# Linear attention on one core: every product as 64x64 quarters of TensorE, four shared double PSUM banks, a new order of the stages

## The chip, the cores and the metric

The kernel runs on one core of one Trainium2 chip. The metric is the device time of one execution in microseconds (us). Four computing engines work side by side: TensorE (PE in the profile, with its weight loads listed apart as PEld), VectorE (DVE), ScalarE (ACT) and GpSimd (POOL). SyncE (SP) issues DMA transfers. Each engine runs its own list of instructions in order and waits on semaphores for the others. TensorE writes its products to PSUM, a small memory of banks; DVE and ACT read PSUM and the larger SBUF.

## The reference

```
def phi(x):
    proj = np.einsum('bhsd,df->bhsf', x, w_phi)
    proj = proj - np.max(np.abs(proj), axis=-1, keepdims=True)
    return np.concatenate([np.exp(proj), np.exp(-proj)], axis=-1)
q_p, k_p = (phi(q), phi(k))
kv = np.einsum('bhsf,bhsd->bhfd', k_p, v)
z = np.sum(k_p, axis=2)
num = np.einsum('bhsf,bhfd->bhsd', q_p, kv)
den = np.einsum('bhsf,bhf->bhs', q_p, z)[..., None] + 1e-06
return (num / den).astype(np.float32)
```

q, k and v are 8 batches x 8 heads x 576 rows x 64 columns, w_phi is 64x128, so a row has 256 features. The attention output is laid out as 4608 tokens x 512 and goes through a mixture of 8 experts (512 to 1024, ReLU, back to 512). Tokens are assigned to experts greedily by descending logit, at most 576 tokens to an expert.

## The kernel before, in words

The attention stage takes about the first 355 us of the execution, the routing the next 45, and the experts the rest. The change touches the attention stage alone.

The stage is cut into 16 **units**, one for each pair of batches (bp) and pair of heads (hp); four units in a row share a pair of batches. A unit's steps, with the names that the text uses and the lines of the profile:

- loads of q, k and v by SP's DMAs (L113), ten in a unit;
- kt and qt: three groups each of three 128x128 transposes of k and q on PE (L165, L243), copied from PSUM to SBUF by ACT (kh at L166, qh at L244);
- kg and qg: three groups each of projections with w_phi, as 64x64 quarters of PE's array (L152). On DVE follow the maximum of the absolute values (km, qm at L156) and the subtraction (ks, qs at L159), on ACT for the keys two exponentials (ke, L177 and L178);
- kv: the key-value products (L189 with 128 rows of the array, L194 with quarters), copied by ACT (L212), then bd, quarter products that lay the result out for the next step and append the gate (L222), copied by ACT (kz, L225);
- the sums over rows of the key features on POOL (L201, L202, L205), then z, their sums over partitions on PE (L234, one column each), copied by DVE into kz (zk, L235);
- T: three groups of six transposes of the query features (L255), then two exponentials on ACT (ex, L258);
- num: four groups of the numerator, the denominator and eight gate columns (L279, 73 columns, in groups of 5, 4, 5 and 4 blocks of rows). On DVE follow what the text calls an x group, x0 to x3: add 1e-6 to the denominators (L283), reciprocals (L284), gate columns (lg, L288), and the output rows (L298). For every fourth unit lg is summed into the logits L (L291, L293). After x3 the rows go out by DMA (L301).

In the last unit the output rows are multiplied by ACT (L296). After every fourth unit but the last come twelve short steps of routing preparation on DVE (L433 to L473, called chores here) and a count on PE (L469). Forty steps that set up routing constants run on DVE and POOL in the first units.

The order of the work is set by a planner, the class Plan: each step is a task with an engine, a duration, a due time, the tasks it depends on, and the buffers it takes and gives back. The planner picks, engine by engine, the ready task with the lowest cost of due time and waiting. It counts a switch between shapes of PE's array as extra time. The due times come from the table ATT. The order is fixed when the kernel is built, and each engine runs it as written.

PSUM holds two double banks D (projections, bd and T), two single banks S (transposes, z, num and the count) and two banks for kv.

Of the kernel before, what the change touches and what calls it, by code (L numbers as in the profile page):

```python
# [17 lines left out]
class Plan:  # L18
# [9 lines left out]
    def order(self):  # L28
# [7 lines left out]
        while left:  # L36
            best=None; horizon={}
            cand={}
            for x in left:
# [4 lines left out]
                if not ok: continue
                for d_ in x['deps']:
                    y=self.by[d_]
                    if 'end' not in y: ok=False; break
                    r=max(r,y['end']+self.SEM if e!='PE' or y['eng']!='PE' else y['start']+y['dur'])
                if not ok: continue
                for kind,n,u in x['slot']:  # L50
                    h=held.setdefault(kind,[0.]*n)
                    z=[t for t in h if t is not None]
                    if not z: ok=False; break
                    r=max(r,min(z)+self.SEM)
                if not ok: continue
                cand.setdefault(e,[]).append((r,x))
# [33 lines left out]
def attention(ctx, tc, nc, q, k, v, w_phi, w_gate, xs, L, C, xp, cfg={}, after=None, later=None, count=None, init=iter(())):  # L90
# [3 lines left out]
    d=dict(TI=21.,kt=-4.,kg=0.,kv=4.,bd=4.,z=5.,zc=6.,qt=6.,qg=10.,T=2.5,num=26.,stay=2.,ks=4.,qs=4.,ns=5.,ng=6,ld=60.,nqP=8,init=25.,pitch=1.)  # L94
# [11 lines left out]
    def load(u,first=lambda: None):
        bp,hp=divmod(u,NP)
        qi=sb.tile([128,2,9,D],F32,name='qi',bufs=2); ki=sb.tile([128,2,9,D],F32,name='ki',bufs=2); vi=sb.tile([128,2,9,D],F32,name='vi',bufs=3)
        T['q',u],T['k',u],T['v',u]=qi,ki,vi
        def put(t,p,s0,s1,x,b,row):  # L110
# [25 lines left out]
    QI=227.  # L136
    def unit(u):
        bp,hp=divmod(u,NP)
        t0=u*d['TI']
# [4 lines left out]
        def slots(*l): return tuple((kd,n,(kd,u) if len(z)==0 else (kd,u)+tuple(z)) for kd,n,*z in l)
        ld0=('ld',)

        def project(x,X,src,i0,i1):
            p=X['p']=bank(X['b'],[128,2,512])(x)
# [12 lines left out]
        for g in range(3):  # L161
            def pe(x,g=g):
                if g==0: T['kh',u]=sb.tile([128,9,128],F32,name='kh',bufs=2)
                p=T['ktp',u,g]=bank(('S',u,'kt',g),[128,3,128])(x)
                for i in range(3): PE.transpose(p[:,i],ch(T['k',u],3*g+i),ident)  # L165
            def act(x,g=g): A.copy(T['kh',u][:,3*g:3*g+3],T['ktp',u,g])  # L166
            due=d['kt']+d['ks']*1.5*g
            add(('kt',g),'PE',327.,due,pe,ld0,'A',slots(('S',NS,'kt',g),*((('kh',2),) if g==0 else ())),(('ki',u),),after=(5500.,9000.,10000.)[g] if u==0 else 0.)
            add(('kh',g),'ACT',ac(384),due+.4,act,(('kt',g),),frees=(('S',u,'kt',g),))
        for g in range(3):  # L170
# [8 lines left out]
            add(('kg',g),'PE',3*QI,due,pe,[('kh',g)],'Q',slots(('D',ND_,'kg',g)),(('kh',u),),after=8000. if u==0 else 0.)  # L179
            add(('km',g),'DVE',dv(768),due+.8,lambda x,X=X: maxima(X,'km',3),(('kg',g),))  # L180
            add(('ks',g),'DVE',dv(768),due+1.4,lambda x,X=X: differ(X,'kt',3),(('km',g),),slot=slots(('ktt',3,g)),frees=(('D',u,'kg',g),))
            add(('ke',g),'ACT',2*ac(768,False),due+2.,act,(('ks',g),),slot=slots(('kP',2)) if g==0 else (),frees=(('ktt',u,g),))
        for g in range(2):
            def pe(x,g=g):
                kP=T['kP',u]; v_=T['v',u]
                if g==0: T['kvps',u]=[ps.tile([128,256],F32,name='kv%d'%i,bufs=1) for i in range(2)]
                for i,b in KV[g]:
                    a,s_=divmod(b,9); c=a^i
                    PE.matmul(T['kvps',u][i][64*c:64*c+64,:],v_[:,a,s_,:],kP[:,b,:],start=b in (0,5,9,14),stop=False,skip_group_check=True)  # L189
                if g==1:  # L190
                    for a in range(2):
                        for i in range(2):
                            c=a^i; r=slice(64*i,64*i+64)
                            PE.matmul(T['kvps',u][i][64*c:64*c+64,:],v_[r,a,4,:],kP[r,9*a+4,:],start=False,stop=True,skip_group_check=True)  # L194
            add(('kv',g),'PE',4*430.+(530. if g==1 else 0.),d['kv']+d['ks']*(2+2.5*g),pe,[('ke',1+g)]+([('kv',0)] if g else []),('B','Q') if g else 'B',slots(('kv',1)) if g==0 else (),(('kP',u),('vi',u)))
# [30 lines left out]
        add(('bd',),'PE',560.,kend+d['bd'],bdp,[('kvt',)],'Q',slots(('D',ND_,'bd')))  # L226
        add(('kz',),'ACT',ac(576),kend+d['bd']+.6,kzc,[('bd',)],frees=(('D',u,'bd'),),slot=slots(('kz',2)))
        def z(x):
            p=T['zp',u]=bank(('S',u,'z'),[128,8])(x)
            for i in range(2):  # L230
                for fh in range(2):
                    for a in range(2):
                        n=4*i+2*fh+(a^i)
                        for e in range(2): PE.matmul(p[64*e:64*e+64,n:n+1],T['ks',u][:,i,a,128*fh+64*e:128*fh+64*e+64],C['one'][:,0:1],start=True,stop=True,skip_group_check=True)  # L234
# [4 lines left out]
        for g in range(3):
            def pe(x,g=g):  # L240
                if g==0: T['qh',u]=sb.tile([128,9,128],F32,name='qh',bufs=2)
                p=T['qtp',u,g]=bank(('S',u,'qt',g),[128,3,128])(x)
                for i in range(3): PE.transpose(p[:,i,:],ch(T['q',u],3*g+i),ident)  # L243
            def act(x,g=g): A.copy(T['qh',u][:,3*g:3*g+3],T['qtp',u,g])  # L244
            due=d['qt']+d['qs']*1.5*g
            add(('qt',g),'PE',327.,due,pe,ld0,'A',slots(('S',NS,'qt',g),*((('qh',2),) if g==0 else ())),(('qi',u),),after=10500. if u==0 else 0.)
            add(('qh',g),'ACT',ac(384),due+.4,act,[('qt',g)],frees=(('S',u,'qt',g),))
        for g in range(3):
# [3 lines left out]
            def tr(x,X=X,g=g):  # L252
                p=X['T']=bank(('D',u,'T',g),[128,2,512])(x)
# [636 lines left out]
```

## Time and profile before

| what | value |
|---|---|
| median of 3 runs | 857.91 us (857.84 to 860.48) |
| the profiled execution's own time | 857.9 us |
| its span | 856.1 us (1.8 us of its time lie around it) |
| granted TensorE clock, mean | 0.978 |
| busy over the span | PE 803.4, DVE 570.2, ACT 370.0, POOL 262.1 us |
| first bd of units 3, 7 and 11 (middle of the stage) | 100.24, 182.31, 264.36 us |
| last num of PE ends | about 355 us |

The three times of bd say that a cycle of four units takes 82.07 and 82.05 us. In the rows of the timeline a line gives the start, the duration, the engine, the line of the kernel, the operation, what is written and read, the shapes, the count (x24 stands for 24 records in a row), and in brackets the idle time of the engine before it and what ended it. A group's line gives busy time and mean duration of one.

### The profile page before, as it was taken

The page shows a single profiled execution, that of the slowest core. Times are in us where ns is not written, and L with a number is a line of the kernel's source. Part 1 is how long each engine was busy: PE and PEld are TensorE (multiplying, and loading weights), DVE is VectorE, ACT ScalarE, POOL GpSimd, SP SyncE. Part 2 cuts the span into 40 slices and gives each one's busy share as a digit, 9 for nine tenths or more (in the row PEclk, how much of TensorE's full clock was granted, in tenths as well). Part 3 has the DMA queues.
Part 4 walks back from the last instruction along what each step waited for, and adds up shares of the span by engine and source line. Part 5 has one row for each costly group of instructions (what it writes and reads, how often), then busy time and mean ns, then how long its engine had stood idle before and what let it go on. Part 6 is the DMA issues. An engine that isn't in the chain of part 4 may idle for free.

```text
span 856.1 us, 24776 instructions
## 1 busy us (share of the span) xinstructions
PE 803.4 (94%) x10508; PEld 685.8 (80%) x10508; DVE 570.2 (67%) x1534; ACT 370.0 (43%) x691; POOL 262.1 (31%) x300
## 2 busy tenths in 40 slices
PE   4879999999999999758999999999999999999995
PEld 2768887887788878658979879889889798898984
DVE  1787788778867887577858658668667577461410
ACT  1646665566566565413334324333333243251410
POOL 1654455555555555111040130310301202401001
PEclk9999999999999999958999999999999999999999
DMA  8424444454445421134143340532233225610301
GB/s 170 116 54 113 114 114 126 118 135 121 117 120 134 117 58 31 57 114 131 54 147 118 129 147 35 177 131 95 97 118 123 83 104 185 214 63 38 118 13 43
DMA packets 73534, 91.88 MB, mean 107 GB/s; under 512 B 5280, under 2 KB 56512, under 8 KB 73424
## 3 DMA queue, kind: packets, MB, share of 16 engines
q1 hardware_dynamic: 67328, 71.32, 29.3%
q0 software_dynamic: 6096, 18.98, 6.5%
q8 instruction: 83, 1.36, 0.7%
q14 instruction: 27, 0.22, 0.1%
HBM read 71.40 MB, written 18.87 MB: 105 GB/s over the span
## 4 chain that ended last, share of the span: by engine, by line
PE 69%; issue 16%; DVE 7%; POOL 4%; DMA 2%; ACT 1%; SPq 0%; POOLq 0%; DVEq 0%; ACTq 0%
PE h L763 19%; PE y L792 16%; PE S L279 7%; PE D L152 6%; PE kv L189 4%; PE D L255 3%; PE y L807 2%; PE S L165 2%; PE S L243 2%; PE h L739 2%; PE S L234 2%; DVE km L156 1%; PE rps L530 1%; POOL out_dram L821 1%; DVE kt L159 1%
## 5 line engine op out<-in xcount | busy, mean ns | idle before, releaser
L763 PE MATMUL h<-xh,w1h 128*128 128x272 f32 (+1 forms) x512 | 145.9, 305 | 0.7 <-ACT xh L740 0.7
L763 PE MATMUL h<-xh,w1l 128*128 128x304 f32 (+1 forms) x512 | 143.9, 301 | 0.0
L774 ACT ACTIVATE fh<-h 128x272 fp32r<-128x272 f32 (+1 forms) x128 | 49.2, 384 | 134.5 <-PE h L763 122.1
L821 POOL DMA_INDIRECT out_dram<-ysb,idx x40 | 40.5, 1012 | 207.0 <-ACT ysb L815 203.5
L792 PE MATMUL y<-w2h,fl 128*128 128x512 f32 x256 | 102.0, 398 | 0.0
L792 PE MATMUL y<-w2l,fh 128*128 128x512 f32 x256 | 101.9, 398 | 0.0
L792 PE MATMUL y<-w2h,fh 128*128 128x512 f32 x256 | 101.5, 396 | 0.0
L763 PEld LDWEIGHTS h<-xh,w1h 128*128 128x128 f32 x512 | 97.2, 190 | 2.5 <-issue 1.2
L763 PEld LDWEIGHTS h<-xh,w1l 128*128 128x128 f32 x512 | 97.4, 190 | 0.0
L734 POOL DMA_INDIRECT xg<-xs,idx x40 | 40.0, 1000 | 178.2 <-issue 141.5
L763 PE MATMUL h<-xl,w1h 128*128 128x272 f32 (+1 forms) x512 | 91.4, 298 | 0.0
L778 DVE SCALAR_TENSOR_TENSOR fl<-h,fh 128x272 fp32r<-128x272 f32 (+1 forms) x128 | 52.8, 419 | 55.6 <-ACT fh L774 41.9
L201 POOL TENSOR_TENSOR ks<-kP 128x512 f32<-128x512 f32 x32 | 40.9, 1277 | 157.1 <-issue 130.2
L279 PE MATMUL S<-kz,qP 128*64 128x73 f32 x2304 | 87.4, 230 | 1.0 <-ACT xp L296 1.0
L279 PEld LDWEIGHTS S<-kz,qP 128*64 128x64 f32 x2304 | 78.1, 137 | 11.0 <-issue 9.1
L202 POOL TENSOR_TENSOR ks<-ks,kP 128x512 f32<-128x512 f32 x64 | 81.5, 1273 | 4.9
L258 ACT ACTIVATE qP<-D 128x768 f32<-128x768 f32 x96 | 72.5, 808 | 9.1 <-PE D L255 5.6
L763 PEld LDWEIGHTS h<-xl,w1h 128*128 128x128 f32 x512 | 75.5, 188 | 0.0
L815 ACT COPY ysb<-y 128x512 f32<-128x512 f32 (+1 forms) x40 | 21.8, 544 | 104.4 <-PE y L792 72.3
L156 DVE TENSOR_REDUCE km<-D 128x6 f32<-128x768 f32 x48 | 45.7, 953 | 29.4 <-PE D L152 29.2
L189 PE MATMUL kv<-kP,vi 128*64 128x256 f32 x512 | 60.9, 379 | 0.0
L156 DVE TENSOR_REDUCE qm<-D 128x6 f32<-128x768 f32 x48 | 45.6, 950 | 20.0 <-PE D L152 19.8
(177 smaller groups left out, 1550.5 us busy)
## 6 DMA issues: line engine op xcount, KB each, us to landing
raww<-in_moe_w_dram SPq DMA_DIRECT2D x64, 512.0 KB, 5.5
qi<-in_q_dram SPq DMA_DIRECT2D x32, 288.0 KB, 4.6
xs<-xp SPq DMA_DIRECT2D x16, 576.0 KB, 3.8
ki<-in_k_dram SPq DMA_DIRECT2D x32, 160.0 KB, 3.8
vi<-in_v_dram SPq DMA_DIRECT2D x32, 160.0 KB, 5.2
ki<-in_k_dram SPq DMA_DIRECT2D x32, 128.0 KB, 3.7
vi<-in_v_dram SPq DMA_DIRECT2D x32, 128.0 KB, 5.0
xg<-xs,idx POOLq DMA_INDIRECT x40, 3.5
```

Of the source, the lines that this page charges most:

```text
L152: PE.matmul(p[64*(c^r):64*(c^r)+64,r,128*(i-i0):128*(i-i0)+128],src[64*r:64*r+64,i,64*(c^r):64*(c^r)+64],C['w'][64*r:64*r+64,:],start=True ...
L156: V.tensor_reduce(m[:,:,0:n],X['v'],axis=AX.X,op=OP.max,apply_absolute_value=True)
L189: PE.matmul(T['kvps',u][i][64*c:64*c+64,:],v_[:,a,s_,:],kP[:,b,:],start=b in (0,5,9,14),stop=False,skip_group_check=True)
L201: if i==0: G.tensor_add(ks[:,:,a],X(0),X(1))
L202: elif i<3: G.tensor_add(ks[:,:,a],ks[:,:,a],X(i+1))
L258: for fh in range(2): A.activation(qP[:,fh].rearrange('p (b i) f -> p b (i f)',b=2),X['T'][:,:,0:384],AF.Exp,scale=1.0-2*fh)
L279: PE.matmul(p[64*ab:64*ab+64,j-j0,:],T['qP',u,jj][:,fh,o,64*ab:64*ab+64],T['kz',u][:,ab,fh,a^ab,:],start=fh==0,stop=fh==1)
L763: PE.matmul(p,ws[:,k,o:o+128],xx[:,k,o1:o2],start=n==0,stop=n==11)
L774: A.activation(hh[:,f,o1:o1+m1],p[:,0:m1],AF.Relu)
L778: V.scalar_tensor_tensor(hl[:,f,o1:o1+m1],p[:,0:m1],0.0,hh[:,f,o1:o1+m1],op0=OP.max,op1=OP.subtract)
L792: PE.matmul(p,hx[:,f,o:o+128],ws[:,f%2,:],start=n==0,stop=n==23)
L821: st=G.indirect_dma_start(out=ov,out_offset=bass.IndirectOffsetOnAxis(ap=iv,axis=0),in_=yv,in_offset=None)
```

## The change

- All transposes, kv, z and num become 64x64 quarter products, as the projections and bd were. A transpose of 128x128 becomes four quarter products with the identity, of 64 columns each (new function turn, L131). A quarter product reads one half of the 128 rows, so where a sum runs over 128 rows the two row halves go to the two banks of a double bank, and are added afterwards.
- For kv, ACT copies one half (kvc, L220) and DVE adds the other (kvt, L223). For z, DVE copies one half and adds the other (L252). For num, ACT copies one half to a new SBUF tile nu (xc, L301), and DVE adds the other half into it (L304).
- The rest of an x group reads nu in SBUF instead of PSUM (L306, L307, L311). The multiplication that gives the output rows goes from DVE to POOL (xa, L320), in the last unit too.
- PSUM is four double banks D0 to D3, which all products share.
- Loads are tasks of their own for k, q and v (L114), where one task issued all ten.
- The planner has new costs and a new table of due offsets for each step, with corrections for the first and the last unit. The order on every engine is new.

The core of the diff:

```
-    ND_,NS=2,2
+    ND_=4
+    def turn(p,g,f):
+        for i in range(3):
+            for c in range(2):
+                for r in range(2): PE.matmul(p[64*c:64*c+64,r,64*i:64*i+64],f(i)[64*r:64*r+64,64*c:64*c+64],ident[64*r:64*r+64,64*r:64*r+64],start=True,stop=True,skip_group_check=True)
...
-                for i in range(3): PE.transpose(p[:,i],ch(T['k',u],3*g+i),ident)
-            def act(x,g=g): A.copy(T['kh',u][:,3*g:3*g+3],T['ktp',u,g])
+                turn(p,g,lambda i: ch(T['k',u],3*g+i))
+            def act(x,g=g): A.copy(rows(T['kh',u][:,3*g:3*g+3]),halves(T['ktp',u,g],3))
...
+                def mm(i,b,r,start,stop):
+                    a,s_=divmod(b,9); c=a^i; z=slice(64*r,64*r+64)
+                    PE.matmul(T['kvps',u][64*c:64*c+64,r,256*i:256*i+256],v_[z,a,s_,:],kP[z,b,:],start=start,stop=stop,skip_group_check=True)
...
+        def kvc(x):
+            T['kvT',u]=sb.tile([128,2,256],F32,name='kvT',bufs=2)
+            A.copy(T['kvT',u].rearrange('p i f -> p (i f)'),T['kvps',u][:,0])
         def kvt(x):
-            kt=T['kvT',u]=sb.tile([128,2,256],F32,name='kvT',bufs=2)
-            for i in range(2): A.copy(kt[:,i],T['kvps',u][i])
+            kt=T['kvT',u].rearrange('p i f -> p (i f)')
+            V.tensor_add(kt,kt,T['kvps',u][:,1])
...
-                                PE.matmul(p[64*ab:64*ab+64,j-j0,:],T['qP',u,jj][:,fh,o,64*ab:64*ab+64],T['kz',u][:,ab,fh,a^ab,:],start=fh==0,stop=fh==1)
+                                for r in range(2):
+                                    h=slice(64*r,64*r+64)
+                                    PE.matmul(p[64*ab:64*ab+64,r,m:m+73],T['qP',u,jj][h,fh,o,64*ab:64*ab+64],T['kz',u][h,ab,fh,a^ab,:],start=fh==0,stop=fh==1,skip_group_check=True)
+                def half(x,n=n,X=X):
+                    X['t']=sb.tile([128,5,73],F32,name='nu',bufs=3)
+                    A.copy(X['t'].rearrange('p j n -> p (j n)')[:,0:73*n],X['p'][:,0,0:73*n])
...
-                    V.tensor_scalar(rd[:,:n],p[:,:n,72:73],1e-6,None,op0=OP.add)
+                    V.tensor_add(f,f,X['p'][:,1,0:73*n])
+                    rd=X['rd']=sb.tile([128,5,1],F32,name='rd',bufs=4)
+                    V.tensor_scalar(rd[:,:n],t[:,:n,72:73],1e-6,None,op0=OP.add)
                     V.reciprocal(rd[:,:n],rd[:,:n])
...
-                    V.tensor_mul(lg[:,j0:j1,:,h],p[:,:n,64:72],rd[:,:n].to_broadcast([128,n,8]))
+                    V.tensor_mul(lg[:,j0:j1,:,h],t[:,:n,64:72],rd[:,:n].to_broadcast([128,n,8]))
...
-                        V.tensor_mul(x_[:,j0:j1,64*a:64*a+64],p[:,:n,0:64],rd[:,:n].to_broadcast([128,n,64]))
+                def pool(x,a=a,j0=j0,j1=j1,n=n,X=X,g=g):
+                    x_=T['x',u]
+                    G.tensor_mul(x_[:,j0:j1,64*a:64*a+64],X['t'][:,:n,0:64],X['rd'][:,:n].to_broadcast([128,n,64]))
...
-ATT = {'TI': 20.56, 'kt': -4.44, 'kg': -1.69, 'kv': 7.48,
...
+ATT = {'TI': 26.229, 'kt': -4.44, 'kg': -1.69, 'kv': 7.48,
...
```

The order shows three places. The first is TensorE at the start of the stage. Names are the tiles written and read: ki_96 and ki_119 are the keys of units 0 and 1 before, ki_97 and ki_113 those after, kh the copied transposes, w the projection weights. Before:

```order
L165 MATMUL S0_132<-ident_69,ki_96 128x128 [waits DMAHW0_49,DMAHW1_49,DVE_49,PE_49]
L165 MATMUL S0_132<-ident_69,ki_96 128x128
L165 MATMUL S0_132<-ident_69,ki_96 128x128 [waits DMAHW3_49,DMAHW2_49]
L165 MATMUL S1_137<-ident_69,ki_119 128x128 [waits DMAHW3_49,DMAHW2_49]
L165 MATMUL S1_137<-ident_69,ki_119 128x128
L165 MATMUL S1_137<-ident_69,ki_119 128x128 [waits DMAHW5_49,DMAHW4_49]
L152 MATMUL D0_143<-w_65,kh_131 64x128 [waits DMASW0_49,Activation_49]
```

And after:

```order
L131 MATMUL D0_119<-ident_69,ki_97 64x64 [waits DMAHW2_49]
L131 MATMUL D0_119<-ident_69,ki_97 64x64 [waits DMAHW3_49]
L131 MATMUL D0_119<-ident_69,ki_97 64x64
L131 MATMUL D1_132<-ident_69,ki_97 64x64 x12
L131 MATMUL D2_146<-ident_69,ki_97 64x64 x12
L160 MATMUL D3_160<-w_65,kh_118 64x128 [waits DMASW0_49,Activation_49]
L160 MATMUL D3_160<-w_65,kh_118 64x128 x11
```

The first projection stood behind transposes of unit 1's keys; now it stands behind transposes of unit 0's keys alone.

The second place is VectorE in the middle of the stage: the last x group of a unit and what follows it. S1 and D1 are PSUM banks, nu, rd, lg and xp are SBUF tiles. Before:

```order
L283 TENSOR_SCALAR rd_2343<-S1_2310 128x4 [waits PE_49]
L284 RECIPROCAL rd_2343<-rd_2343 128x4 [waits DVE_49]
L288 TENSOR_TENSOR lg_2033<-S1_2310,rd_2343 128x32 [waits DVE_49]
L298 TENSOR_TENSOR xp_2032<-S1_2310,rd_2343 128x4x64
L156 TENSOR_REDUCE km_2364<-D1_2330 128x6 [waits PE_49]
```

And after, with the end of the x group before it:

```order
L311 TENSOR_TENSOR lg_5802<-nu_7021,rd_7059 128x40 [waits DVE_49]
L304 TENSOR_TENSOR nu_7081<-nu_7081,D1_7023 128x292 [waits Activation_49]
L306 TENSOR_SCALAR rd_7097<-nu_7081 128x4 [waits DVE_49]
L307 RECIPROCAL rd_7097<-rd_7097 128x4 [waits DVE_49]
L311 TENSOR_TENSOR lg_5802<-nu_7081,rd_7097 128x32 [waits DVE_49]
L164 TENSOR_REDUCE km_7136<-D2_7104 128x6 [waits PE_49]
L167 TENSOR_TENSOR kt_7178<-D2_7104,km_7136 128x2x3x128 [waits DVE_49]
```

The x groups of a unit now stand one behind the other, their operands are SBUF tiles but for the bank of the first add, and the multiplication is gone from this engine.

At the same place GpSimd had only the sums of the key features (ks and kP are SBUF tiles):

```order
L201 TENSOR_TENSOR ks_2382<-kP_2227 128x2x256 [waits PE_49,Activation_49,Pool_49]
L202 TENSOR_TENSOR ks_2382<-ks_2382,kP_2227 128x2x256 [waits Pool_49] x2
L205 TENSOR_TENSOR ks_2382<-ks_2382,kP_2227 64x256 [waits Pool_49]
L205 TENSOR_TENSOR ks_2382<-ks_2382,kP_2227 64x256
L201 TENSOR_TENSOR ks_2382<-kP_2227 128x2x256 [waits Activation_49,Pool_49]
```

And it has now, in the unit of the VectorE rows above:

```order
L210 TENSOR_TENSOR ks_6911<-ks_6911,kP_6766 128x2x256 [waits Pool_49]
L320 TENSOR_TENSOR xp_6997<-nu_6947,rd_6994 128x5x64 [waits DMAHW2_49,DVE_49]
L320 TENSOR_TENSOR xp_6997<-nu_6999,rd_7003 128x4x64 [waits DVE_49]
L320 TENSOR_TENSOR xp_6997<-nu_7021,rd_7059 128x5x64 [waits DVE_49]
L210 TENSOR_TENSOR ks_6911<-ks_6911,kP_6766 128x2x256 [waits Pool_49]
L320 TENSOR_TENSOR xp_6997<-nu_7081,rd_7097 128x4x64 [waits DVE_49]
L213 TENSOR_TENSOR ks_6911<-ks_6911,kP_6766 64x256 [waits Pool_49] x2
```

The four multiplications stand between the sums. On TensorE at this place, after the last num of the unit (D3, kz, qP), the rows run:

```order
L298 MATMUL D3_7606<-kz_7101,qP_7304 64x73 x31
L234 MATMUL D0_7647<-bd_103,kvT_7444 64x72 [waits DVE_49]
L131 MATMUL D1_7667<-ident_69,qi_6538 64x64 [waits Activation_49]
L160 MATMUL D2_7689<-w_65,kh_7122 64x128 [waits DVE_49]
L131 MATMUL D0_7708<-ident_69,ki_6660 64x64 [waits Activation_49]
L131 MATMUL D3_7723<-ident_69,ki_6660 64x64 [waits DVE_49]
L131 MATMUL D1_7737<-ident_69,qtt_7328 64x64 [waits Activation_49]
L160 MATMUL D0_7768<-w_65,kh_7707 64x128 [waits Activation_49]
L131 MATMUL D3_7785<-ident_69,ki_6660 64x64 [waits Activation_49]
L131 MATMUL D2_7800<-ident_69,qtt_7343 64x64 [waits DVE_49]
```

These are the first instructions of num3's remainder, bd, a qt, a kg, two kt, a T, a kg, a kt and a T; rows that follow each in the same bank are left out. The bank D2 of the last T was that of the kg six rows above it.

More of the change, by code (lines that the diff above doesn't have):

```diff
@@ L49, in order @@
                 if not ok: continue
+                want={}
                 for kind,n,u in x['slot']:
[L51 to L54, printed above, removed]
+                    h=held.setdefault(kind,[0.]*n); i=want[kind]=want.get(kind,-1)+1
+                    z=sorted(t for t in h if t is not None)
+                    if i>=len(z): ok=False; break
+                    r=max(r,z[i]+self.SEM)
                 if not ok: continue
@@ L74, in order @@
                 m0=x['mode'][0]
-                if mode[0] not in (None,m0): s+=95.
-                if mode[0]!=m0 or s>free.get(e,0.)+1.: s+=100. if m0=='A' else 50.
+                if mode[0] not in (None,m0): s+=self.swc
+                if mode[0]!=m0 or s>free.get(e,0.)+1.: s+=self.swA if m0=='A' else self.swO
                 mode[0]=x['mode'][-1]
@@ L101, in attention, with load, put @@
     w=sb.tile([128,512],BF,name='warm',bufs=1); V.memset(w,0.0)
-    p=ps.tile([128,512],F32,name='S0',bufs=1)
-    for _ in range(cfg.get('nwarm',7)): PE.matmul(p,w[:,0:128],w,start=True,stop=True)
+    p=ps.tile([128,2,512],F32,name='D0',bufs=1)
+    for _ in range(cfg.get('nwarm',7)): PE.matmul(p[:,0],w[:,0:128],w,start=True,stop=True)
     T={}
     HS=S*D
[L106 to L110, printed above, removed]
+    def load(u,n,first=lambda: None):
+        bp,hp=divmod(u,NP); b=2*bp
+        x=dict(q=q,k=k,v=v)[n]
+        t=T[n,u]=sb.tile([128,2,9,D],F32,name=n+'i',bufs=3 if n=='v' else 2)
+        def put(p,s0,s1,b,row):
             n=s1-s0
@@ L241, in pe, with act @@
                 if g==0: T['qh',u]=sb.tile([128,9,128],F32,name='qh',bufs=2)
-                p=T['qtp',u,g]=bank(('S',u,'qt',g),[128,3,128])(x)
-                for i in range(3): PE.transpose(p[:,i,:],ch(T['q',u],3*g+i),ident)
-            def act(x,g=g): A.copy(T['qh',u][:,3*g:3*g+3],T['qtp',u,g])
+                p=T['qtp',u,g]=bank(('D',u,'qt',g))(x)
+                turn(p,g,lambda i: ch(T['q',u],3*g+i))
+            def act(x,g=g): A.copy(rows(T['qh',u][:,3*g:3*g+3]),halves(T['qtp',u,g],3))
             due=d['qt']+d['qs']*1.5*g
-            add(('qt',g),'PE',327.,due,pe,ld0,'A',slots(('S',NS,'qt',g),*((('qh',2),) if g==0 else ())),(('qi',u),),after=10500. if u==0 else 0.)
-            add(('qh',g),'ACT',ac(384),due+.4,act,[('qt',g)],frees=(('S',u,'qt',g),))
+            add(('qt',g),'PE',3*QT,due,pe,[*lq]+[('qt',g-1)]*(g>0),'Q',slots(('D',ND_,'qt',g),*((('qh',2),) if g==0 else ())),(('qi',u),))
+            add(('qh',g),'ACT',ac(384),due+.4,act,[('qt',g)],frees=(('D',u,'qt',g),))
         for g in range(3):
@@ L301, in dve @@
                         nc.sync.dma_start(o,x_)
-                add(('num',a,g),'PE',n*270.,due,pe,[('zk',)]+[('ex',j) for j in js],'B',slots(('S',NS,'num',a,g)),tuple(('qP',u,j) for j in js)+(('kz',u),))
-                add(('x',a,g),'DVE',70+70+dv(8*n)+(dv(64*n) if u<NU-1 else 0)+(250 if hp==NP-1 else 0),due+1.6,dve,[('num',a,g)],frees=(('S',u,'num',a,g),))
+                add(('num',a,g),'PE',n*270.,due,pe,[('zk',)]+[('ex',j) for j in js],'Q',slots(('D',ND_,'num',a,g)),tuple(('qP',u,j) for j in js)+(('kz',u),))
+                add(('xc',a,g),'ACT',ac(73*n),due+1.2,half,[('num',a,g)],slot=slots(('nu',3,a,g)))
+                add(('x',a,g),'DVE',dv(73*n)+70+70+110+8*n+(250 if hp==NP-1 else 0),due+1.6,dve,[('xc',a,g)]+[('x',*divmod(i-1,2))]*(i>0)+[('x',1,1,u-1)]*(i==0 and hp>0),frees=(('D',u,'num',a,g),))
+                add(('xa',a,g),'POOL',150+2.*64*n,due+2.,pool,[('x',a,g)]+[('xa',*divmod(i-1,2))]*(i>0),frees=(('nu',u,a,g),))
         if hp==NP-1 and u<NU-1:
```

114 lines of the change are left out of this document (58 added, 56 removed).

## The prediction

> **What bounds the kernel now.** I read the busy time by stretches first, then the chain of waits, then the timeline of one unit. The first rows are the middle of the attention stage (PE, PEld, DVE, ACT, POOL, each with its busy us and count) and the chain's shares by engine.
>
> ```profile
> 60.00:340.00 280.00, 273.97 (x5922) 228.87 (x5924) 222.53 (x478) 175.26 (x287) 143.19 (x136) 1.00 0.43 108
> PE 69%; issue 16%; DVE 7%; POOL 4%; DMA 2%; ACT 1%; SPq 0%; POOLq 0%; DVEq 0%; ACTq 0%
> ```
>
> PE is busy 273.97 of 280 us at full clock; DVE is busy 222.53, so 79%, POOL 51%. The stage is bound by PE with DVE not far behind. The next rows are PE in one unit, start and duration first.
>
> ```profile
> 80.54 0.68 PE L222 MATMUL D<-bd,kvT 64*64 64x72 f32 x32
> 81.15 1.10 PE L234 MATMUL S<-one,ks 128*64 128x1 f32 x32
> 82.17 0.89 PE L152 MATMUL D<-w,kh 64*64 64x128 f32 x24
> 82.99 0.55 PE L165 MATMUL S<-ident,ki 128*128 128x128 f32 x3
> 83.38 0.49 PE L243 MATMUL S<-ident,qi 128*128 128x128 f32 x3
> 83.70 0.82 PE L255 MATMUL D<-ident,qtt 128*128 128x128 f32 x6
> 84.45 1.24 PE L279 MATMUL S<-kz,qP 128*64 128x73 f32 x32
> 85.61 0.89 PE L152 MATMUL D<-w,kh 64*64 64x128 f32 x24
> 86.32 0.83 PE L152 MATMUL D<-w,qh 64*64 64x128 f32 x24
> 87.09 1.49 PE L279 MATMUL S<-kz,qP 128*64 128x73 f32 x40
> 88.40 1.90 PE L189 MATMUL kv<-kP,vi 128*64 128x256 f32 x16
> 90.23 0.55 PE L243 MATMUL S<-ident,qi 128*128 128x128 f32 x3
> ...
> 95.41 0.66 PE L194 MATMUL kv<-kP,vi 64*64 64x256 f32 x8
> 95.89 0.83 PE L152 MATMUL D<-w,kh 64*64 64x128 f32 x24
> ...
> 100.24 0.55 PE L222 MATMUL D<-bd,kvT 64*64 64x72 f32 x24
> 162.61 0.68 PE L222 MATMUL D<-bd,kvT 64*64 64x72 f32 x32
> ```
>
> From bd to bd this unit takes 100.24 - 80.54 = 19.70 us, and four units 162.61 - 80.54 = 82.07. So a cycle has 82.07 - 4x19.70 = 3.27 us more, which go with the chores of its last unit. Durations overlap at their ends, so I price by start to start.
>
> **The change on PE.** A projection behind another of the same shape takes 86.32 - 85.61 = 0.71, ahead of a num 87.09 - 86.32 = 0.77, and ahead of transposes 82.99 - 82.17 = 0.82. The 32 records of num ahead of a projection take 1.16, where the 40 ahead of kv (same shape) take 1.31, which makes 1.05 of 32. So a switch of shape costs 0.06 to 0.11, say 0.10. I count 13 in the unit; with one shape they all go, 1.3 us.
>
> The price of a quarter comes from bd: 16 products in 0.61, 0.51 without its switch, so 0.127 for four quarters of 72 columns. Num becomes 36 such fours, 4.6; its rows give 2x1.31 + 2x1.05 = 4.7. Three transposes become three fours of 64 columns, at most 0.38; rows 0.39 and 0.32. A T of six becomes at most 0.76; row 0.75. L189's 16 records (eight half-array products) take 1.83 with a switch, 0.43 for two, so 3.87 for nine fours of 256 columns against 2x1.83 + 0.48 = 4.14 with switches. Z goes from 32 records to 64: by bd's 0.51/32 = 16 ns a record it takes 1.0, by its own present 1.02/32 = 32 ns a record 2.0. I take 1.0, since bd's shape is the new one. PE's own work per unit: 6x0.37 + 3x0.75 + 6x0.71 + 3.87 + 0.51 + 1.0 + 4.6 = 18.7. That agrees with 19.70 - 1.3 = 18.4. I take 18.6; the bounds are 18.4 and 19.4 (z at its present rate). The quarters gain the switches and little else.
>
> **The change on DVE.** It loses the multiplication of four x groups and gains four adds, kvt and a second zk. These rows give the prices, by the spacing of starts.
>
> ```profile
> 87.45 0.95 DVE L156 TENSOR_REDUCE qm<-D 128x6 f32<-128x768 f32 x1
> 88.31 0.95 DVE L159 TENSOR_TENSOR kt<-D,km 128x768 f32<-128x768 f32 x1
> 89.18 0.95 DVE L159 TENSOR_TENSOR qtt<-D,qm 128x768 f32<-128x768 f32 x1
> 90.04 0.16 DVE L283 TENSOR_SCALAR rd<-S 128x5 f32<-128x5 f32 x1
> 90.23 0.19 DVE L284 RECIPROCAL rd<-rd 128x5 f32<-128x5 f32 x1
> 90.46 0.23 DVE L288 TENSOR_TENSOR lg<-S,rd 128x40 f32<-128x40 f32 x1
> 90.58 0.48 DVE L298 TENSOR_TENSOR xp<-S,rd 128x320 f32<-128x320 f32 x1
> ```
>
> 768 elements take 0.87 where nothing is waited for, and about 0.1 more where a maximum is followed by its own subtraction. The add of 365 or 292 elements lies between L288 and L159, about 0.45 or 0.37 by size; with 0.19 + 0.23 + 0.23 for the rest, an x group of five or four takes 1.09 or 0.99. Kvt with 512 elements is 0.58.
>
> Now the loop that can set the pace. Between the end of a unit's last qg and the T that waits for bank D2, DVE in its new order has qm, kvt, qs, four x groups, km and ks: 1.0 + 0.58 + 0.87 + 2x1.09 + 2x0.99 + 1.0 + 0.95 + 0.15 for the signal = 8.7. PE has four nums, bd, two qt, two kg, three kt and a T there: 4.6 + 0.51 + 5x0.37 + 2x0.71 + 0.75 = 9.1. That kg on D2 needs the add of x2, and the T needs the ks of that kg, so PE can't run ahead of DVE. The rest of the unit is 18.6 - 9.1 = 9.5 of PE. A unit is thus 9.5 plus the longer of 9.1 and 8.7 + c, where c is what DVE waits inside that chain. At c = 0 PE sets it, 18.6.
>
> **What c is.** The x groups read SBUF now, and POOL, which had only sums, has four multiplications more, which fall among them. The rows show what a DVE instruction with SBUF operands does beside POOL.
>
> ```profile
> 108.71 2.63 POOL L202 TENSOR_TENSOR ks<-ks,kP 128x512 f32<-128x512 f32 x2
> 110.16 0.23 DVE L288 TENSOR_TENSOR lg<-S,rd 128x40 f32<-128x40 f32 x1
> 110.70 0.73 DVE L293 SCALAR_TENSOR_TENSOR L<-L,lg 128x40 f32<-128x40 f32 x1
> 111.42 1.53 POOL L205 TENSOR_TENSOR ks<-ks,kP 64x256 f32<-64x256 f32 x2
> 114.38 2.63 POOL L202 TENSOR_TENSOR ks<-ks,kP 128x512 f32<-128x512 f32 x2
> 116.08 1.00 DVE L293 SCALAR_TENSOR_TENSOR L<-L,lg 128x32 f32<-128x32 f32 x1
> 117.08 1.51 POOL L205 TENSOR_TENSOR ks<-ks,kP 64x256 f32<-64x256 f32 x2
> 121.03 0.23 DVE L293 SCALAR_TENSOR_TENSOR L<-L,lg 128x40 f32<-128x40 f32 x1
> ...
> 132.10 1.66 POOL L205 TENSOR_TENSOR ks<-ks,kP 64x256 f32<-64x256 f32 x2
> 133.10 0.70 DVE L449 TENSOR_SCALAR dg<-di 128x9 bf16<-128x9 int32 x1
> ...
> 356.95 0.16 DVE L449 TENSOR_SCALAR dg<-di 128x9 bf16<-128x9 int32 x1
> ```
>
> L293 has two SBUF inputs. Beside L202 it takes 0.73 and 1.00, and both times it ends as L202 ends (110.70 + 0.73 = 111.43, and 108.71 + 2.63 = 111.34; 117.08 and 117.01). With POOL idle the same shape takes 0.23. L449, a scalar operation from SBUF to SBUF, takes 0.70 beside L205 and 0.16 alone. L288, with one input in PSUM, takes 0.23 beside L202. So a DVE instruction of the first two kinds that meets a POOL instruction waits for its end. In the new x group these are L306 (was from PSUM) and L311 (was PSUM and SBUF).
>
> The Trainium skill states this rule ("SBUF — State Buffer", Who interferes with whom): the port pair that DVE shares with GpSimd is held for a whole instruction, two SBUF inputs contend for it, and the scalar form too where it takes both ports. The rows agree. By that rule, as by the rows, the change puts eight such instructions into each unit.
>
> POOL's durations are 2.63/2 = 1.3 for 512 elements and 1.53/2 = 0.75 for 256, so about 0.87 and 0.75 for the multiplications of 320 and 256. Its busy time per unit becomes 2x(3x1.3 + 2x0.75) + 2x(0.87 + 0.75) = 14.0, 70% of a unit. The multiplication of a group starts when its reciprocal is done and about as its lg ends, and the next group's L306 comes 0.45 to 0.5 later, behind the add: a wait of 0.3 to 0.4 in three of the groups and 0.3 behind a sum in the first, 1.3 together. Between the third and fourth multiplication stands a sum of 1.3; if it starts between L306 and L311 of x3, L311 waits 1.1, and I count half, 0.5. So c = 1.8. Below, it is 0 if nothing overlaps; above, 3 and more if several L311 wait for a sum. The unit then takes 9.5 + 8.7 + 1.8 = 20.0, 0.3 more than now.
>
> **The start, the chores, the tail.**
>
> ```profile
> 9.19 0.45 PE L165 MATMUL S<-ident,ki 128*128 128x128 f32 x1 [1.67 <-DMA ki<-in_k_dram]
> ...
> 15.64 0.66 PE L165 MATMUL S<-ident,ki 128*128 128x128 f32 x2 [6.00 <-DMA ki<-in_k_dram]
> ...
> 17.34 1.56 PE L152 MATMUL D<-w,kh 64*64 64x128 f32 x24
> 18.96 0.96 DVE L156 TENSOR_REDUCE km<-D 128x6 f32<-128x768 f32 x1 [14.60 <-PE D L152]
> ```
>
> PE waited 6.00 us for unit 1's keys ahead of the first projection, and DVE began at 18.96. In the new order nothing of unit 1 stands there. With unit 0's keys in at 9.19, the copy (0.5) and the projection follow, and DVE begins at about 11: -8. It is up to -10 if early waits for loads go too, and only -3 if the values, now issued behind both queries and unit 1's keys, hold kv back. Loads are ten issues on SP as before, and in the middle PE waits for none of the rows above.
>
> The chores and L293 fall into DVE's chain, which has no slack left: for a cycle I take 6 us in place of 3.27, from four L293 at up to 1.00, and two L291 and twelve short steps beside them. Over the three cycles with chores that is +8 (0 if they find gaps, +13 if each waits as L449 did). At the end, the last output rows come by a copy, an add and a POOL multiplication in place of ACT's: +2 (0 to 4). The copies of num's halves go to ACT, which is busy 175.26 of 280: four a unit at no more than L298's 0.48 each add 1.9 to some 12.3, and are covered; the add of a group starts that much later, which the order allows for by putting other work of DVE ahead of it.
>
> Sum, against the profiled execution's 857.9 (which is the median 857.91): -8 + 14x0.3 + 8 + 2 = +6, so 864. The break-even is where 14x(18.2 + c - 19.70) = -2, at c = 1.36. A measurement of this kernel can tell about 0.3%, 2.6 us.
>
> **The rivals.**
> - No wait to speak of (the other side, faster). If POOL runs in DVE's PSUM instructions, or few of the eight meet it, c stays under 0.4 and PE sets the pace at 18.6 to 18.8. Then -8 + 14x(18.7 - 19.70) + 4 + 2 = -16: 842, from 838 to 846. For it: no row shows L306 in this place, and an instruction may slip in between two of POOL's. Against: POOL at 70%. Chance 0.22.
> - Half of it: only L311 waits, or L306 alone, c = 1.0. The unit is 19.2, and the sum -8 - 7 + 7 + 2 = -6: 852, from 848 to 856. It decides below c = 1.36. Chance 0.20.
> - More of it: several L311 behind sums, c = 3. The unit is 21.2: -8 + 21 + 9 + 2 = +24, 882. For it: L293 waited 0.5 and 0.8 in two cases of three. Chance 0.14.
> - The change doesn't do what it says on PE: small quarters are bound by issue, not by columns. Z has 32 ns a record with one column now, bd 16 with 72. Turns, num and z are 288 + 288 + 64 = 640 records in the new unit, 10.2 us at bd's rate. At the mean of the two rates, 24 ns, they take 15.4, the unit 18.6 + 5.1 = 23.7, and the sum is -8 + 56 + 8 + 2 = +58: 916. Bd's own 32 records of quarters speak against it, so its chance is 0.05. The Trainium skill ("TensorE: Matmul & The Clock Gate", Back-to-back issue gap) puts a floor of about 25 ns under the spacing for up to 64 columns; by it the same sum gives an estimate of about 925. Bd's 0.61/32 = 19 ns, its switch included, lies below that floor.
>
> **How the numbers follow.** The forecast, c from 1.4 to 2.4, has 0.39 and a range of 858 to 872. Faster by over 0.3% (under 855.3) takes all of the first rival and 0.16 of the second: 0.38. Within 0.3% (855.3 to 860.5) takes the rest of the second, 0.04, and 0.08 of the forecast: 0.12. Slower takes 0.50. The range leaves out the last rival and the outer parts of the first and third: 838 to 882. The likeliest case's own range, since cases of both signs hold most of the chance, is 858 to 872.
>
> **What would show it.** Right: bd to bd about 20.0 in units without chores, PE waiting for DVE ahead of a T or kg, L306 or L311 at several times 0.16 and 0.23 and ending with a POOL instruction, no switch costs (a projection at 0.71 everywhere), the first DVE maximum near 11 us. Wrong: L306 and L311 near their old 0.16 and 0.23 (then the first rival), PE busy the whole unit at over 19 us (then the quarters cost more), or waits of PE for ACT or DMAs, which no term here has.

## The result and the profile after

The changed kernel takes 964.75 us (962.7 to 966.36, four runs) against 858.13 us, a ratio of 1.1234 with an interval of 1.1204 to 1.1265. (Every ratio below, too, is to runs of the kernel before that were made beside it.) That is slower by 107 us and far outside the stated range. The profiled execution took 965.38 us with a span of 963.6.

The whole loss lies in the attention stage: the last num of PE starts at 460.14 us of the span where it started at 354.75, and from there to the end it is 503.4 us against 501.4. The first row is a stretch of the changed kernel's attention stage, in the columns of the prediction.

```profile
60.00:440.00 380.00, 281.42 (x11972) 259.87 (x11968) 242.02 (x498) 195.25 (x323) 178.53 (x191) 0.96 0.29 79
```

From its page, the queue that loads instructions (packets, MB, share) and the chain's shares:

```profile
q8 instruction: 140, 2.29, 1.0%
PE 67%; issue 22%; DVE 6%; POOL 3%; DMA 1%; ACT 1%; SPq 0%; POOLq 0%; DVEq 0%; ACTq 0%
```

PE is busy 281.42 of 380 us, 74%, where it was 98%. No other engine is busier than it was: DVE 64%, POOL 47%. So no engine is full, and yet hardly a wait for another engine stands in the profile: the waits of PE in the same stretch (total, times, longest) name "issue", which is time in which the engine waited for nothing that the profile shows.

```profile
PE D L131 <- issue: 35.1, 18, 3.0
PE D L160 <- issue: 29.2, 20, 2.8
PE D L298 <- issue: 26.5, 21, 2.1
PE D L197 <- issue: 2.0, 2, 1.3
```

That is 93 us in 61 stops, most of them of 1 to 3 us. Over the whole attention stage it is 108 us, as much as the kernel lost; in the kernel before it was 0.2. The granted clock in this stretch was 0.96 against 1.00 in the middle of the kernel before; the run wide_turn below has 0.99 there and takes as long, so the clock isn't the cause. The timeline of PE shows where they fall.

```profile
193.32 1.92 PE L298 MATMUL D<-kz,qP 64*64 64x73 f32 x105 [1.37 <-issue]
195.03 0.52 PE L131 MATMUL D<-ident,qi 64*64 64x64 f32 x22
197.22 0.21 PE L131 MATMUL D<-ident,qi 64*64 64x64 f32 x1 [1.68 <-issue]
197.23 0.29 PE L298 MATMUL D<-kz,qP 64*64 64x73 f32 x3
197.28 0.22 PE L131 MATMUL D<-ident,qi 64*64 64x64 f32 x1
197.33 1.18 PE L298 MATMUL D<-kz,qP 64*64 64x73 f32 x61
198.30 0.71 PE L234 MATMUL D<-bd,kvT 64*64 64x72 f32 x32
198.80 0.56 PE L131 MATMUL D<-ident,qi 64*64 64x64 f32 x24
199.14 0.43 PE L160 MATMUL D<-w,kh 64*64 64x128 f32 x6
200.95 0.70 PE L160 MATMUL D<-w,kh 64*64 64x128 f32 x17 [1.37 <-issue]
```

The stops fall in the middle of groups, where no step begins or ends. Between the stop at 197.22 and that at 200.95 stand 1 + 3 + 1 + 61 + 32 + 24 + 6 = 128 records; between 193.32 and 197.22 it is 105 + 22 = 127. Each record has its own weight load, so this is 256 instructions. The instruction queue moved 2.29 MB in 140 packets, 16 KB each, and PE's 2 x 17868 instructions make 139.6 blocks of 256. The kernel before had 83 packets, and 2 x 10508 / 256 = 82.1:

```profile
q8 instruction: 83, 1.36, 0.7%
```

The packets of that queue beside the stops, all from the trace of the changed kernel:

```
code load, us         PE's last product begins            PE goes on
190.65 to 191.78      191.72                              193.32
194.45 to 195.77      195.32                              197.22
198.33 to 199.74      199.31                              200.95
203.42 to 204.69      203.28                              206.05
207.20 to 208.19      208.17                              209.67
```

PE goes on 1.2 to 1.5 us after a load has ended, and the next load begins about 1.1 us later, in all but one of the rows. With 1.0 to 1.4 us for the load itself that makes a loop of some 3.8 us, one block at a time. All 62 stops of over 0.8 us in the attention stage lie like that: PE goes on 1.2 to 1.7 us after the end of a load, and from one stop to the next there are one to five times 128 records, less up to 5 (other instructions may take places in a block). In the attention stage of the changed kernel the loads follow each other at a median of 3.83 us, the closest 5% at under 3.48. In the kernel before the median is 5.73 and the closest 3.55.

### The profile page after: what moved, and what is told of

The parts are those of the page before. It is cut to its first block, busy times and chain, and to the rows that moved or that the text cites. A ratio compares the mean times of both kernels' runs of the same rounds, so it can differ in the third digit from the quotient of the medians.

```text
span 963.6 us, 39526 instructions
## 1 busy us (share of the span) xinstructions
PE 815.1 (85%) x17868; PEld 726.5 (75%) x17868; DVE 600.1 (62%) x1570; ACT 393.0 (41%) x721; POOL 303.9 (32%) x364
## 3 DMA queue, kind: packets, MB, share of 16 engines
q8 instruction: 140, 2.29, 1.0%
## 4 chain that ended last, share of the span: by engine, by line
PE 67%; issue 22%; DVE 6%; POOL 3%; DMA 1%; ACT 1%; SPq 0%; POOLq 0%; DVEq 0%; ACTq 0%
PE h L787 17%; PE y L816 14%; PE D L298 8%; PE D L131 8%; PE D L160 7%; PE D L197 5%; PE y L831 2%; PE h L763 2%; PE rps L554 1%; POOL out_dram L845 1%; PE D L249 1%; PE D L234 1%; PE rps L550 1%; DVE qm L164 1%; DVE qtt L167 1%
## 5 line engine op out<-in xcount | busy, mean ns | idle before, releaser
L298 PE MATMUL D<-kz,qP 64*64 64x73 f32 x4608 | 90.4, 229 | 33.7 <-issue 32.1
L298 PEld LDWEIGHTS D<-kz,qP 64*64 64x64 f32 x4608 | 83.2, 137 | 38.6 <-issue 36.9
L197 PE MATMUL D<-kP,vi 64*64 64x256 f32 x1152 | 72.9, 383 | 2.0 <-issue 2.0
L160 PE MATMUL D<-w,kh 64*64 64x128 f32 x1152 | 50.2, 280 | 21.9 <-issue 21.7
```

Source lines behind the costliest of these rows:

```text
L160: PE.matmul(p[64*(c^r):64*(c^r)+64,r,128*(i-i0):128*(i-i0)+128],src[64*r:64*r+64,i,64*(c^r):64*(c^r)+64],C['w'][64*r:64*r+64,:],start=True ...
L197: PE.matmul(T['kvps',u][64*c:64*c+64,r,256*i:256*i+256],v_[z,a,s_,:],kP[z,b,:],start=start,stop=stop,skip_group_check=True)
L298: PE.matmul(p[64*ab:64*ab+64,r,m:m+73],T['qP',u,jj][h,fh,o,64*ab:64*ab+64],T['kz',u][h,ab,fh,a^ab,:],start=fh==0,stop=fh==1,skip_group_che ...
```

## The experiments

The theory: code is the bound. A block of 128 products with their weight loads comes every 3.8 us at best, and where PE runs through it faster it stands still for the rest. The rivals: the wait theory of the forecast (DVE behind POOL sets the pace), and an array theory (the quarters are slow in the array itself).

**Transposes whole again (full_turn).** The order stays that of the changed kernel; the kt, qt and T steps issue one record for 128x128 in place of eight.

```
-                turn(p,g,lambda i: ch(T['k',u],3*g+i))
+                for i in range(3): PE.transpose(p[:,0,128*i:128*i+128],ch(T['k',u],3*g+i),ident)
(qt and T alike, with their copies)
```

> All transposes (kt, qt and T) are 128x128 again, one record each in place of eight, in the order of the changed kernel; the rest is as changed. TensorE's records per unit fall from 890 to about 638. Code theory (TensorE stands still every 128 products because a block of 256 instructions, 16 KB, takes about 3.8 us to come): the stops in the transposes go and those in the nums stay, so about 250 of 890 products fewer: 870 to 905 us. Wait theory (VectorE's waits behind GpSimd in the x groups set the pace): nothing on VectorE or GpSimd changes, 955 to 970. Array theory (quarters are slow in the array): a gain of the time between records alone, with no stops of over a microsecond left or right, 900 to 940.

Measured: 894.75 us, ratio 1.0428 (1.0398 to 1.0458). Records per unit fall from 890 to 638, stops are left at the quarter nums and behind them (the stretch from 60 to 380 us):

```profile
PE D L298 <- issue: 28.9, 23, 2.6
PE D L234 <- issue: 6.4, 7, 1.1
PE D L260 <- DVE nu L304: 1.0, 1, 1.0
```

The code theory holds, the wait theory doesn't: DVE and POOL do the same work in the same order, and 70 us are gone. The eight records in place of one are four quarters times two: a product in f32 leaves two records here (bd has 16 products and 32 records), a transpose left one.

**Half of that (full_kq).** Only kt and qt whole, T in quarters.

> Only kt and qt are 128x128 transposes again, T stays in quarters: about 764 records per unit, half of what full_turn takes away. Code theory: half of full_turn's gain, 915 to 935, with stops again exactly 128 products apart. Wait theory: 955 to 970.

Measured: 924.62 us, ratio 1.0776 (1.0745 to 1.0807), with 764 records per unit. Half of the records gave 40 of the 70 us. The stops again lie whole multiples of 128 records apart, less up to 6.

**More columns, the same instructions (wide_turn).** Each quarter transpose streams the identity twice.

```
-p[64*c:64*c+64,r,64*i:64*i+64], ... ident[64*r:64*r+64,64*r:64*r+64]
+p[64*c:64*c+64,r,64*i:64*i+128], ... ident[64*r:64*r+64,64*r:64*r+64][:,None,:].to_broadcast([64,2,64])
```

> Each quarter transpose streams 128 columns in place of 64 (the identity twice, the second copy is overwritten or not read); the number of instructions and the order are those of the changed kernel. By the projections' 0.71 us for 24 records that is 72 fours a unit at 0.235 in place of 0.127, so 7.8 us more of the array a unit, 125 us in all. Code theory: 128 such products take 3.8 us in place of 2.0, which the loads of code cover, so 960 to 995. Array theory (time goes with columns streamed): 1075 to 1095. Wait theory: VectorE's chain stays, PE's own work becomes 26.4 a unit, 960 to 1000.

Measured: 962.63 us, against 964.75 of the changed kernel. The stretch from 60 to 440 us, and then the waits of PE in it (total, times, longest):

```profile
60.00:440.00 380.00, 321.53 (x12119) 301.86 (x12119) 241.98 (x505) 199.00 (x325) 180.01 (x193) 0.99 0.29 79
```

```profile
PE D L298 <- issue: 24.6, 21, 1.7
PE D L131 <- issue: 21.0, 15, 3.5
PE D L160 <- issue: 9.8, 12, 1.6
PE D L197 <- issue: 1.0, 1, 1.0
```

PE is busy 40 us longer in the same 380 us, the stops have shrunk from 93 to 56 us, and the time is the same. The expectation counted too much: 288 records of transposes are 36 fours of eight records, not 72, so by its own prices the array gets 3.9 us more a unit, 62 in all. If the array set the pace, the kernel would take some 1027 us in place of 1075 to 1095, still far from 962.63. The array had that much room, so the array theory falls. The wait theory, which isn't excluded here, had fallen with full_turn: the pace is set by the number of instructions.

**Num alone whole (full_num).** Num over all 128 rows, 144 records fewer per unit, and no add of a second half; the transposes stay quarters.

> The changed kernel with num alone over all 128 rows again (144 records a unit fewer, one bank, no add on VectorE); the transposes stay quarters. About 746 records a unit. Code theory: what counts is the number of instructions in dense stretches, not which product they belong to, so it lies near full_kq with its 764: 905 to 930, with stops in the transposes and projections and none in the nums. If the nums in quarters were slow in themselves, as full_turn_num against full_turn could also be read, it would lie at 965 - 44 = 921 as well; the place of the stops then tells: none may be left in the transposes.

Measured: 896.88 us, ratio 1.0447 (1.0417 to 1.0478). The stops are in the transposes and the projections beside them, at the nums almost none, in the whole stage 2.1 us (the largest rows from 60 to 380 us):

```profile
PE D L131 <- issue: 27.8, 19, 3.0
PE D L160 <- issue: 4.0, 4, 1.5
PE D L131 <- DVE kt L167: 2.0, 3, 0.8
```

The place of the stops is as expected, the time is lower than expected by 8 us and more, and 28 us under full_kq with nearly the same number of records (746 and 764). So the count over a whole unit isn't the measure by itself: in the whole attention stage PE's issue stops are 43 us in full_num and 54 in full_kq, and PE is busy 333.6 and 349.0 us. The two make up 26 of the 28 us. That full_num also leaves out DVE's adds of the second half may be part of it; how much wasn't tried.

**Both whole (full_turn_num).**

> As full_turn, and num as products over all 128 rows again, 144 records a unit in place of 288, in one bank; ACT copies the whole result and VectorE's add of the second half (L304) is left out, since there is none. kv, z, projections and bd stay in quarters, loads and order as changed. About 494 records a unit. Code theory: a block of 128 products takes over 3.8 us nearly everywhere, the stops all but go, and what is left is PE's own 19 to 20 us a unit with the early start: 845 to 870. Wait theory: the waits of L306 and L311 stay, four adds of 0.45 go, 925 to 950.

Measured: 850.65 us, ratio 0.9907 (0.9863 to 0.9952), faster than the kernel before. Issue is gone from PE's waits, of which these three rows are all between 60 and 340 us, and the pace is 19.60 us from bd to bd in units without chores.

```profile
PE D L272 <- DVE kt L167: 3.3, 3, 1.1
PE D L490 <- DVE cmp L489: 1.7, 3, 0.7
PE D L272 <- DVE qtt L167: 1.0, 1, 1.0
```

**The multiplication back on DVE, in the changed kernel (x_on_dve).** The planner has it as a task of DVE, so it also plans the order anew, with small differences.

```
-                    G.tensor_mul(x_[:,j0:j1,64*a:64*a+64],...)
+                    V.tensor_mul(x_[:,j0:j1,64*a:64*a+64],...)
```

> The changed kernel with the multiplication of the output rows back on VectorE (reading nu and rd in SBUF), so GpSimd has the sums alone. VectorE gets 64 instructions of 0.45 more, all else as changed. Code theory: nothing moves, 955 to 972. Wait theory, the one of the forecast (VectorE behind GpSimd's multiplications sets the pace): a unit loses most of its waits and gains 1.8 of work on VectorE; if the waits had been the cause of the 107 us, over 50 of them go: under 915.

Measured: 969.45 us, ratio 1.1304 (1.125 to 1.1357). Taking POOL's multiplications away gains nothing here, so they weren't the cause of the 107 us. The stops stay, from 60 to 440 us above all:

```profile
PE D L160 <- issue: 31.5, 21, 3.5
PE D L298 <- issue: 28.8, 23, 1.9
PE D L131 <- issue: 28.3, 14, 3.3
```

**The same where code doesn't set the pace (fast_x_dve).**

> full_turn_num with the multiplication of the output rows on VectorE. There code no longer sets the pace, and L303 and L308 wait 2.1 us a unit behind GpSimd. If these waits count on the path, as the forecast had it, taking away the multiplications' part of them (about half) and adding 1.8 us of work on VectorE gives 0 to +1 us a unit: 850 to 866. If TensorE alone sets the pace of 19.6, no change: 848 to 853.

Measured: 877.61 us, ratio 1.0233 (1.0215 to 1.025), 27 us more than full_turn_num and more than either expectation. DVE got 64 instructions of 0.48 or 0.42 us, 29 us in all, and the time grew by nearly as much; the order is planned anew here too, so the two aren't separated. PE waits for DVE now ("kt L167" 10.7 us and chores among them). The waits of the x groups did not go:

```profile
L308 DVE TENSOR_TENSOR lg<-nu,rd 128x40 f32<-128x40 f32 x24 | 15.7, 656 | 0.8
L303 DVE TENSOR_SCALAR rd<-nu 128x4 f32<-128x4 f32 x24 | 12.4, 517 | 0.0
L303 DVE TENSOR_SCALAR rd<-nu 128x5 f32<-128x5 f32 x24 | 10.1, 422 | 3.2 <-ACT nu L299 3.2
L308 DVE TENSOR_TENSOR lg<-nu,rd 128x32 f32<-128x32 f32 x24 | 9.5, 395 | 0.8
```

In the kernel before the same steps took 157 and 232 or 217 ns:

```profile
L288 DVE TENSOR_TENSOR lg<-S,rd 128x40 f32<-128x40 f32 x28 | 6.5, 232 | 1.0
L288 DVE TENSOR_TENSOR lg<-S,rd 128x32 f32<-128x32 f32 x27 | 5.9, 217 | 0.9
L283 DVE TENSOR_SCALAR rd<-S 128x5 f32<-128x5 f32 x28 | 4.4, 157 | 8.1 <-PE S L279 8.1
```

With no multiplication on POOL they still take 1.8 to 3.3 times as long. They wait behind POOL's sums, which had always been there: of these 96 instructions 44 are drawn out (L303 to over 0.2 us, L308 to over 0.28), and each of the 44 ends within 0.1 us after the end of a sum. What exposes them is that their operands moved from PSUM to SBUF, as the next run shows.

**Operands back in PSUM (fast_psum).** As full_turn_num, but L303 and L308 read the bank.

```
-                    t=X['t']; f=t.rearrange('p j n -> p (j n)')[:,0:73*n]
+                    t=X['p'][:,0,0:73*n].rearrange('p (j n) -> p j n',n=73)
```

> full_turn_num with L303 and L308 of the x groups reading the bank in PSUM in place of the copy nu in SBUF; GpSimd's multiplication still reads nu. The planner's order is the same, but a num's bank comes free after VectorE and not after ACT's copy. Wait theory in the regime where code does not set the pace: both take 0.16 and 0.22 again, the 2.1 us of waits per unit go. If they lay on the path: 825 to 846. If TensorE's 19.6 sets the pace: 848 to 853. If the later release of the banks counts: over 853.

Measured: 844.56 us (841.34 to 845.68, five runs), ratio 0.9832 (0.9812 to 0.9852), the fastest of the study. The waits are gone (the groups of L303 and L308), and PE is full (the stretch from 60 to 340 us):

```profile
L308 DVE TENSOR_TENSOR lg<-D,rd 128x40 f32<-128x40 f32 x29 | 6.7, 232 | 1.0
L308 DVE TENSOR_TENSOR lg<-D,rd 128x32 f32<-128x32 f32 x29 | 6.3, 217 | 1.0
L303 DVE TENSOR_SCALAR rd<-D 128x5 f32<-128x5 f32 x30 | 4.8, 160 | 12.9 <-ACT nu L299 12.6 <-POOL xp L317 0.4
L303 DVE TENSOR_SCALAR rd<-D 128x4 f32<-128x4 f32 x29 | 4.5, 156 | 9.9 <-ACT nu L299 9.9
```

```profile
60.00:340.00 280.00, 277.65 (x6993) 236.20 (x6987) 206.89 (x458) 194.96 (x327) 178.55 (x193) 0.99 0.37 100
```

Bd to bd is 19.60 in units without chores, as in full_turn_num; the gain lies in the units with logits and chores. A cycle of four takes 19.60 + 20.08 + 19.76 + 19.60 = 79.0 us, in full_turn_num 19.60 + 21.41 + 20.34 + 19.60 = 81.0, in the kernel before 82.07.

**Steps of one shape together (fast_grouped).** full_turn_num with the planner told of three shapes.

> full_turn_num with the planner told of the shapes (transposes, half-array nums and quarters as three kinds), so that steps of one shape stand together: 169 switches of shape in the attention stage in place of 257. At the forecast's 0.10 a switch TensorE saves 8.8 us: 838 to 846 if TensorE sets the pace and the new order waits for nothing else; 850 or more if VectorE or the banks take its place. Code: 494 records a unit, as in full_turn_num, no stops.

Measured: 921.7 us, ratio 1.0753 (1.0732 to 1.0775), 76 us above the range for a pace set by TensorE; the other branch, VectorE or the banks in its place, is what came. Issue stops are 2.4 us in all. With four nums in a row and the projections behind them, PE waits for DVE before the kv ("OH L481" 6.9, "kt L167" 6.1 us), the projections ("qtt L167" 6.7) and the transposes ("kt L167" 4.3); a unit without chores takes 22.6 us and more. What the fewer switches are worth can't be seen under this.

**The early start alone (start_alone).** The kernel before, with unit 1's key transposes held back.

```
-...,after=(5500.,9000.,10000.)[g] if u==0 else 0.)
+...,after=(5500.,9000.,10000.)[g] if u==0 else 17000. if u==1 else 0.)
```

> The kernel before, with unit 1's key transposes kept from standing ahead of unit 0's first projection (a release time in the planner; the order of unit 0 and 1 changes, nothing else). The forecast gave the start 8 us (3 to 10). If an earlier start of VectorE is carried to the end: 848 to 855. If the loads of the values or TensorE's order in unit 1 take it back: 856 to 860.

Measured: 854.88 us (852.62 to 857.28, six runs), ratio 0.9971 (0.9955 to 0.9986). DVE's first maximum begins at 10.40 in place of 18.96 us, and in the profiled execution, the fastest of the six, the last unit's bd at 337.84 in place of 344.76, so 6.9 earlier. In that execution 1.7 of it is lost again after the last num (503.0 us to the end against 501.4). The median shows 2.8; what differs between executions wasn't tried.

## Why the prediction was wrong, point by point

- **What bounds the kernel.** Right for the kernel before, and for the changed one the step that failed. The forecast made the unit "9.5 plus the longer of 9.1 and 8.7 + c", times of the array and of DVE. It left out how PE gets its instructions. The trace of the kernel before had what it takes to ask: 83 packets of 16 KB on the instruction queue, and none closer than 3.55 us to the one before. The change takes PE from 430 records per unit to 890, so from 3.4 blocks of 256 instructions to 7.0; at the forecast 20.0 us that would be one every 2.9 us, closer than any two had been. At 3.83 it is 26.6 us a unit; what was measured is 28.2 on average from the bd of unit 2 to that of unit 12.
- **The quarters' price in the array.** Right as far as rows within a block show. The 32 records of bd and the nums around them run as priced (bd starts 198.30, the next group 198.80, so 0.50; 105 num records in 1.71 us, 16 ns each). Right prices summed to a wrong pace, because the array wasn't the bound.
- **Issue-bound quarters**, the rival at 0.05 and 916 us, had the right direction, fewer instructions being better, but not the mechanism: records inside a block come at 16 ns, and the loss is whole stops of 1 to 3 us every 128. Its working took the spacing of records where it should have taken blocks.
- **The switches of shape.** The forecast gave 13 of them 1.3 us a unit, 0.10 each. Their price is borne out: where no stop falls in between, 24 records of a projection take 0.71 us ahead of transposes and 0.69 ahead of nums (medians of 19 and 5 cases in the changed kernel), against 0.77 to 0.82 ahead of another shape before. What it is worth to the whole stays open: full_turn_num and fast_psum kept switches, and fast_grouped, planned for fewer, changed more than that.
- **What c is.** The mechanism was right and in this kernel it counts for little. Here L306 and L311 take:

```profile
L311 DVE TENSOR_TENSOR lg<-nu,rd 128x40 f32<-128x40 f32 x26 | 7.7, 297 | 0.9
L306 DVE TENSOR_SCALAR rd<-nu 128x5 f32<-128x5 f32 x26 | 7.3, 282 | 0.9
L311 DVE TENSOR_TENSOR lg<-nu,rd 128x32 f32<-128x32 f32 x26 | 5.6, 217 | 0.9
L306 DVE TENSOR_SCALAR rd<-nu 128x4 f32<-128x4 f32 x26 | 5.5, 213 | 0.9
```

  Above the 157, 232 and 217 ns of before that is 2x(125 + 65 + 0 + 56) ns = 0.5 us a unit, not 1.8, in a unit so long that POOL is idle half of it. Where code doesn't slow it down, the same instructions wait as forecast; in full_turn_num:

```profile
L308 DVE TENSOR_TENSOR lg<-nu,rd 128x40 f32<-128x40 f32 x28 | 15.9, 567 | 1.0
L303 DVE TENSOR_SCALAR rd<-nu 128x4 f32<-128x4 f32 x27 | 15.0, 554 | 2.5 <-ACT nu L299 2.5
L308 DVE TENSOR_TENSOR lg<-nu,rd 128x32 f32<-128x32 f32 x27 | 10.5, 391 | 0.9
L303 DVE TENSOR_SCALAR rd<-nu 128x5 f32<-128x5 f32 x28 | 8.1, 289 | 5.1 <-ACT nu L299 5.1
```

  2x(335 + 397 + 174 + 132) ns = 2.1 us a unit. Of the 54 that are drawn out, 26 end just after a multiplication of POOL and 28 just after a sum. But taking the waits away gained 6 us over the whole stage (850.65 against 844.56), not 1.8 a unit, and having the multiplications on POOL, which the forecast blamed, saves 27 us there (fast_x_dve). The Trainium skill's rule on the shared ports ("SBUF — State Buffer", Who interferes with whom) agrees with these rows, down to the part that one input in PSUM frees the instruction: 567 to 232 ns.
- **The start.** About right: DVE begins at 11.94 in place of 18.96, 7.0 earlier where 8 was forecast. What that is worth at the end is less: alone, in the kernel before, 2.8 us of the median (start_alone).
- **Chores and tail.** The chores can't be told apart from the stops in the changed kernel. Without the stops, a cycle with logits and chores has 81.0 - 4x19.60 = 2.6 us more than four plain units (3.27 before, 6 forecast). DVE's chain had room there; but that kernel also leaves out the four adds of a unit, so it doesn't show the forecast's 6 wrong for the chain as changed. In the changed kernel the time from the last num to the end is 2.1 us longer, where 2 was forecast.

## What to carry to other kernels

Count the instructions that a change adds to TensorE, not only its busy time: divide them by 256 per block, divide the time of the stage by the blocks, and compare with the closest spacing of instruction loads that the profile shows. Splitting products into smaller ones that the array does in the same time can double the code and make code the bound; then adding columns changed nothing here, and fewer, larger instructions in the dense stretches changed much. Stops of TensorE that the profile puts down to "issue", in the middle of a group and at equal counts of instructions, are its mark.

## What the runs showed of the hardware

- TensorE's instructions come in blocks of 16 KB, 256 instructions, and no two loads in the attention stages of the two kernels begin less than 3.3 us apart (median 3.83 in the changed one). The transfer itself takes 0.9 to 1.6 us of that (median 1.16 in the changed kernel). The Trainium skill ("Runtime: NRT & Kernel Launch", Instruction fetch mechanics) has the blocks and calls their cost mostly hidden; the blocks agree, the cost doesn't: here it is 108 us.
- A second block doesn't seem to be loaded ahead while one load is awaited: a dense stretch of two to three blocks stops at every one of them (193.32, 197.22, 200.95), and a load begins only about 1.1 us after PE has gone on. What limits it to one wasn't tried.
- A small VectorE instruction with two inputs in SBUF can be held until a GpSimd instruction ends: L308 took 567 ns on average in full_turn_num, and 232 again with one of the inputs in PSUM (fast_psum).
